# Chunked attention and a gated MLP in one kernel: all turned-block copies placed behind the sigmoid, and a new written order of the opening

## The chip, the cores and the metric

One NeuronCore of a Trainium2 chip. The metric is the device time of one launch in microseconds (us), as the median of several runs; the profile is of one more launch, which has its own time.

## The reference

Inputs are q, k, v of shape (8, 8, 576, 64) and three weights. Attention is within chunks of 64 tokens; its output, as 4608 tokens of 512 numbers, goes through a gated layer.

```python
scores = scale * np.matmul(q_c, k_c.transpose(0, 1, 2, 4, 3))      # chunks of 64 tokens
scores = scores - np.max(scores, axis=-1, keepdims=True)
attn = np.exp(scores)
attn = attn / (np.sum(attn, axis=-1, keepdims=True) + 1e-09)
x = np.matmul(attn, v_c)                                           # then (4608, 512)
gate = 1.0 / (1.0 + np.exp(-(x @ w_gate)))                         # (4608, 1536)
val = x @ w_val
return (gate * val @ w_out).astype(np.float32)
```

## The kernel before, in words

The 4608 tokens are 9 blocks of 512. Blocks 0 to 2 go through the gated layer tile by tile; blocks 3 to 8 go in three pairs with fewer products per pair (the functions from `product` to `outward`), and are not touched here. The hidden size 1536 is 12 tiles of 128. Each block has two attention pairs; a pair covers 256 tokens, with u in {0, 1} naming its two halves and i in {0, 1} the two heads side by side.

Numbers are kept in two parts, high and low (`hi`, `lo`, or `h` and `l`), each of TensorE's fast 32-bit type; a product is three passes. The weights arrive as 64-bit floats and are converted on the chip: ScalarE's `a` (two scalings, L145 and L146), VectorE's `t`, `b`, `d` (L148, L150, L153), ScalarE's `h` (L155), VectorE's `l` (L159), for gate (part 0), value (part 1), both at once (part u, "wide") or output weights (part 2) of tile f. A weight load is `w.f.part` (L118), 512 KB on SP's queue. Staging buffers are shared: a later load waits until the conversion of an earlier one has read its buffer.

**Opening.** Block 0 and the first two tiles of block 1 follow a written order, the string OPENING. Each token is one step, and every engine and SP's queue take their instructions in that order (`begin`). `q.p`, `v.p` load queries and keys (two DMAs) and values of pair p. `scores.p` are the products of pair p; `max`, `neg`, `sub` are VectorE's, and there are two ways to the exponential: `exp` is one ScalarE activation behind VectorE's `sub` and in front of VectorE's `sum`; `each` (L263) is eight activations with the maximum as bias and their sums read out, so that neither `sub` nor `sum` is needed. `inv` and `mul` scale. `turn.p.u` transposes on TensorE, `ca`, `ce` (ScalarE) or `cd` (VectorE) copy half of a turned block out (L287), `av.p` multiplies with the values (L211), `xh` (ScalarE) and `xl` (VectorE) split the result into x. `fill.n` are n products of no use, which keep TensorE busy (L101). `G.n.s` and `V.n.s` are gate and value products of tile n (n counts through the blocks, 12 per block) for tokens a (first half), b (second) or f (all), `g` is the sigmoid, `m` the gating product, `hh` and `hl` the two parts of the hidden tile, `D` its product with the output weights.

**Blocks 1 and 2.** `rest` calls `step` for each tile: `hidden` issues the gate products, the sigmoid (L372), the value products, VectorE's product `hf` (L375), ScalarE's cast `hx` (L378) and VectorE's remainder (L380). `finish` issues the output product of the tile before. Between them a planner, `tick` and `insert`, walks through the generator `flow`, which has the attention of later pairs: its items have a price, and move on as credit is given per tile. A pair's exponentials are one activation (L787), and its blocks are turned by VectorE (L814) in pieces that 16 copies of 32 x 256 (L825) put in place: 5 on POOL at once, and 11 for ScalarE into the list `held`. `release` issues what is held:

```python
    def release(most=16):
        for one in held[:most]:
            one()
        del held[:most]
```

It is called in `hidden` behind the sigmoid, with 5, and behind the cast `hx`, with all that are left; `insert` calls it too, ahead of `av` (`values2`, L211). VectorE also adds weights for the later pairs (L451, `keep_sums`), POOL works on (L460 to L465), SP stores. The finished block's output is copied by VectorE and ScalarE (L409, L407) and sent (L410).

Of the kernel before, what the change touches and what calls it, by code (L numbers as in the profile page):

```python
# [26 lines left out]


OPENING = """
w.1.1 w.0.0 q.0 w.0.1 q.1 w.1.0 a.1.1 v.0 a.0.0 t.1.1 b.1.1 t.0.0 d.1.1 b.0.0 h.1.1 fill.21 scores.0 d.0.0 l.1.1  # L30
h.0.0 max.0.0 a.0.1 neg.0.0 max.0.1 each.0.0 neg.0.1 l.0.0 t.0.1 fill.11 scores.1 b.0.1 each.0.1 inv.0.0 mul.0.0
max.1.0 max.1.1 a.1.0 d.0.1 neg.1.0 sub.1.1 w.2.1 each.1.0 w.0.2 inv.0.1 w.2.0 mul.0.1 w.1.2 t.1.0 fill.17 turn.0.1
q.2 b.1.0 turn.0.0 cd.0.1 ca.0.1 cd.0.0 ca.0.0 inv.1.0 exp.1.1 av.0 d.1.0 h.0.1 sum.1.1 h.1.0 v.1 l.0.1 xh.0.0.1
xh.0.1.0 w.3.0 xl.0.0.1 xh.0.1.1 xh.0.0.0 xl.0.1.1 a.0.2 xl.0.0.0 xl.0.1.0 inv.1.1 fill.9 G.0.a a.2.u mul.1.1 l.1.0
V.0.a mul.1.0 t.0.2 b.0.2 turn.1.0 d.0.2 turn.1.1 g.0.a ca.1.0 G.1.a m.0.a w.2.2 ce.1.0 t.2.u w.3.1 ca.1.1 ce.1.1
b.2.u hh.0.a av.1 h.0.2 a.1.2 l.0.2 V.1.a hl.0.a xh.1.0.1 t.1.2 xh.1.1.1 xl.1.0.1 g.1.a D.0.a xl.1.1.1 xh.1.0.0
xh.1.1.0 m.1.a xl.1.0.0 hh.1.a xl.1.1.0 a.3.u hl.1.a G.0.b d.2.u b.1.2 V.0.b g.0.b h.2.u d.1.2 t.3.u G.1.b w.3.2
h.1.2 w.4.1 m.0.b l.2.u hh.0.b w.4.0 a.2.2 V.1.b l.1.2 hl.0.b D.1.a b.3.u g.1.b a.3.2 m.1.b G.2.f d.3.u hh.1.b
hl.1.b w.5.0 h.3.u t.2.2 w.5.1 b.2.2 a.4.u D.0.b l.3.u d.2.2 scores.2 t.3.2 g.2.f t.4.u V.2.f h.2.2 b.4.u a.5.u
d.4.u G.3.f m.2.f w.6.0 max.2.0 w.6.1 h.4.u q.3 max.2.1 hh.2.f l.4.u V.3.f hl.2.f sub.2.1 g.3.f t.5.u b.3.2 G.4.f  # L40
m.3.f exp.2.1 b.5.u a.6.u sum.2.1 neg.2.0 D.1.b d.3.2 each.2.0 inv.2.1 w.5.2 mul.2.1 V.4.f d.5.u l.2.2 h.3.2 w.7.1
hh.3.f w.7.0 inv.2.0 mul.2.0 v.2 D.2.f h.5.u w.4.2 l.3.2 hl.3.f a.5.2 l.5.u turn.2.0 t.6.u D.3.f b.6.u g.4.f a.7.u
m.4.f t.5.2 b.5.2 G.5.f hh.4.f d.6.u a.4.2 hl.4.f h.6.u d.5.2 V.5.f t.4.2 w.7.2 h.5.2 l.6.u w.8.0 g.5.f ce.2.0 b.4.2
ca.2.0 l.5.2 G.6.f m.5.f d.4.2 hh.5.f t.7.u w.6.2 h.4.2 w.8.1 hl.5.f a.7.2 turn.2.1 l.4.2 D.5.f b.7.u ca.2.1 ce.2.1
g.6.f d.7.u a.6.2 av.2 t.7.2 b.7.2 h.7.u t.6.2 D.4.f b.6.2 a.8.u l.7.u d.6.2 V.6.f d.7.2 w.8.2 h.6.2 t.8.u w.9.2
h.7.2 l.6.2 xh.2.0.1 xh.2.1.1 b.8.u xh.2.1.0 xh.2.0.0 G.7.f m.6.f d.8.u hh.6.f a.8.2 hl.6.f w.10.1 V.7.f l.7.2 w.9.0
g.7.f w.10.0 xl.2.0.0 h.8.u w.9.1 xl.2.1.0 xl.2.1.1 w.11.1 l.8.u D.6.f m.7.f xl.2.0.1 hh.7.f t.8.2 hl.7.f a.9.0
b.8.2 D.7.f t.9.0 b.9.0 d.9.0 a.9.1 d.8.2 G.8.f h.9.0 w.10.2 t.9.1 h.8.2 v.3 l.9.0 b.9.1 a.9.2 d.9.1 V.8.f g.8.f
t.9.2 l.8.2 h.9.1 l.9.1 b.9.2 a.10.0 scores.3 d.9.2 m.8.f h.9.2 G.9.f t.10.0 hh.8.f b.10.0 d.10.0 l.9.2 h.10.0 V.9.f
hl.8.f a.10.1 l.10.0 max.3.1 a.10.2 t.10.1 b.10.1 D.8.f g.9.f t.10.2 b.10.2 d.10.2 d.10.1 w.11.0 h.10.2 G.10.f m.9.f  # L50
q.4 h.10.1 l.10.2 hh.9.f l.10.1 a.11.1 hl.9.f neg.3.1 V.10.f t.11.1 g.10.f b.11.1 a.11.0 d.11.1 t.11.0 w.11.2 h.11.1
b.11.0 D.9.f d.11.0 m.10.f each.3.1 l.11.1 max.3.0 V.11.f sub.3.0 h.11.0 inv.3.1 hh.10.f l.11.0 exp.3.0 hl.10.f
a.11.2 G.11.f sum.3.0 inv.3.0 t.11.2 mul.3.0 mul.3.1 D.10.f b.11.2 d.11.2 g.11.f h.11.2 m.11.f turn.3.0 l.11.2
hh.11.f G.12.a ca.3.0 hl.11.f cd.3.0 turn.3.1 g.12.a D.11.f ca.3.1 cd.3.1 av.3 v.4 ev.1 ev.2 ev.0 ev.3 V.12.a
xh.3.1.1 xh.3.0.1 xl.3.1.1 xh.3.1.0 xl.3.0.1 xh.3.0.0 G.13.a xl.3.0.0 m.12.a xl.3.1.0 hh.12.a hl.12.a V.13.a g.13.a
G.12.b m.13.a hh.13.a hl.13.a V.12.b g.12.b D.12.a m.12.b V.13.b hh.12.b hl.12.b D.12.b G.13.b D.13.a g.13.b m.13.b
hh.13.b hl.13.b
"""

# [933 lines left out]
```

## Time and profile before

| what | value |
|---|---|
| three runs | 901.86, 905.09, 906.74 us; median 905.09 |
| the profiled execution, its own time | 902.03 us |
| its span | 900.2 us |
[...]
| TensorE busy | 98% of the span |
| VectorE, ScalarE, POOL busy | 69%, 46%, 30% |

The span is from the first to the last recorded instruction. Engines are PE (TensorE), PEld (its weight loads), DVE (VectorE), ACT (ScalarE), POOL (GpSimd) and SP, whose queue issues the DMAs. In a row of a timeline, like instructions that follow each other are merged; the us are from the first start to the last end, and the bracket is the engine's idle time before the row with what ended it. "L825" is line 825 of the kernel.

### The profile page before, as it was taken

What the parts mean: (1) busy time and instruction counts of PE and PEld (TensorE: products, weight loads), DVE (VectorE), ACT (ScalarE), POOL (GpSimd) and SP (SyncE); (2) the same over time, 40 slices, a digit from 0 to 9 for tenths busy, and PEclk for the clock granted to TensorE, in tenths of its full rate; (3) what the DMA queues carried; (4) which work ended last, traced back from release to release, by engine and by line L of the source; (5) the groups of instructions that cost most, each with busy time, mean ns of one, the idle gap of its engine ahead of it and who ended that gap; (6) DMA issues with size and microseconds to landing.
All of it is one profiled execution on the core that took longest, in us unless ns stands there. A gap on an engine that the chain in (4) does not pass through costs nothing.

```text
span 900.2 us, 15612 instructions
## 1 busy us (share of the span) xinstructions
PE 882.1 (98%) x6054; PEld 720.3 (80%) x6054; DVE 618.8 (69%) x882; ACT 412.0 (46%) x738; POOL 272.4 (30%) x337
## 2 busy tenths in 40 slices
PE   7999999999999999999999999999999999999998
PEld 4887788887877878888888888887788888888886
DVE  6999882586665966666658976666679853435884
ACT  7887672355524463355544524455246221122341
POOL 0000000397846990267750001253500002432000
PEclk9999999999998999999999999999999999999999
DMA  8899962336354475588775567665446685564553
GB/s 312 305 338 297 353 195 71 131 129 190 131 166 148 142 221 177 171 278 284 257 277 187 210 231 283 234 234 190 163 160 224 211 283 197 183 204 150 187 210 117
DMA packets 84506, 189.77 MB, mean 211 GB/s; under 512 B 7248, under 2 KB 45648, under 8 KB 80592
## 3 DMA queue, kind: packets, MB, share of 16 engines
q1 hardware_dynamic: 84432, 188.77, 61.2%
q8 instruction: 48, 0.79, 0.4%
q14 instruction: 26, 0.21, 0.1%
HBM read 146.28 MB, written 42.47 MB: 210 GB/s over the span
## 4 chain that ended last, share of the span: by engine, by line
PE 81%; DVE 7%; ACT 4%; POOL 3%; issue 2%; DMA 2%; SPq 0%; POOLq 0%; DVEq 0%; ACTq 0%
PE d L699 19%; PE g L356 16%; PE cy L550 15%; PE cx L550 11%; PE cz L550 10%; PE acc L391 7%; PE av L211 2%; PE sc L196 2%; DMA w_raw<-w_in 2%; POOL pt L825 1%; ACT early L263 1%; ACT pt L825 1%; POOL a_val L465 1%; DVE xc L540 1%; DVE w_raw L153 1%
## 5 line engine op out<-in xcount | busy, mean ns | idle before, releaser
L356 PE MATMUL g<-xt,w 128*128 128x512 f32 (+1 forms) x960 | 208.1, 372 | 1.0 <-ACT hf L312 0.5
L356 PEld LDWEIGHTS g<-xt,w 128*128 128x128 f32 x960 | 168.5, 190 | 34.1 <-ACT hf L312 1.5
L699 PE MATMUL d<-hd,wd 128*128 128x512 f32 x756 | 172.5, 389 | 0.1
L699 PEld LDWEIGHTS d<-hd,wd 128*128 128x128 f32 x756 | 141.7, 188 | 30.3 <-DVE hd L679 0.9
L550 PE MATMUL cy<-xc,wr 128*128 128x512 f32 x648 | 159.4, 389 | 1.2 <-DVE s1u L568 1.2
L550 PEld LDWEIGHTS cy<-xc,wr 128*128 128x128 f32 x648 | 121.6, 188 | 26.8 <-DVE s1u L568 1.6
L550 PE MATMUL cx<-xc,wr 128*128 128x512 f32 x432 | 111.0, 392 | 0.6 <-issue 0.6
L550 PE MATMUL cz<-xc,wr 128*128 128x512 f32 x432 | 110.0, 390 | 0.2
L391 PE MATMUL acc<-w,hx 128*128 128x512 f32 x432 | 106.7, 394 | 0.1
L550 PEld LDWEIGHTS cz<-xc,wr 128*128 128x128 f32 x432 | 80.9, 188 | 17.8 <-issue 1.0
L550 PEld LDWEIGHTS cx<-xc,wr 128*128 128x128 f32 x432 | 80.5, 188 | 18.0 <-issue 1.0
L391 PEld LDWEIGHTS acc<-w,hx 128*128 128x128 f32 x432 | 79.7, 188 | 17.7 <-DVE hx L322 0.8
L825 POOL COPY pt<-pr 32x256 f32<-32x256 f32 x94 | 39.7, 423 | 163.9 <-DVE pr L814 154.8
L460 POOL TENSOR_TENSOR a_val<-a_val 128x128 f32<-128x128 f32 x36 | 19.0, 527 | 217.9 <-DVE a_val L451 167.5
L678 ACT CAST hd<-hid 128x1024 fp32r<-128x1024 f32 x48 | 49.9, 1052 | 49.2 <-PE d L699 33.2
L566 ACT COPY s1u<-cx 128x512 f32<-128x512 f32 x36 | 21.1, 587 | 106.3 <-PE cx L550 106.3
L679 DVE TENSOR_TENSOR hd<-hid,hd 128x1024 fp32r<-128x1024 f32 x48 | 58.3, 1221 | 12.4 <-ACT hd L678 12.2
L578 POOL TENSOR_TENSOR hid<-u,hid 128x512 f32<-128x512 f32 x15 | 19.3, 1285 | 142.4 <-DVE u L607 141.7
L825 ACT COPY pt<-pr 32x256 f32<-32x256 f32 x130 | 52.4, 403 | 10.5 <-DVE pr L814 8.6
L568 DVE TENSOR_TENSOR s1u<-cy,s1u 128x512 f32<-128x512 f32 x36 | 24.7, 685 | 39.9 <-PE cy L550 35.4
L628 ACT ACTIVATE hid<-hid 128x512 f32<-128x512 f32 x54 | 32.4, 628 | 35.3 <-DVE hid L622 29.3
L578 POOL TENSOR_TENSOR hid<-s1u,hid 128x512 f32<-128x512 f32 x30 | 41.1, 1379 | 20.8 <-DVE s1u L622 20.2
(118 smaller groups left out, 1118.4 us busy)
## 6 DMA issues: line engine op xcount, KB each, us to landing
wr<-sums SPq DMA_DIRECT2D x72, 512.0 KB, 4.8
wd<-stream SPq DMA_DIRECT2D x30, 1024.0 KB, 4.6
w_raw<-w_in SPq DMA_DIRECT2D x36, 512.0 KB, 5.2
wr<-given SPq DMA_DIRECT2D x36, 512.0 KB, 3.8
qt<-q_in SPq DMA_DIRECT2D x18, 512.0 KB, 4.8
kt<-k_in SPq DMA_DIRECT2D x18, 512.0 KB, 5.7
vt<-v_in SPq DMA_DIRECT2D x18, 512.0 KB, 4.7
given<-w SPq DMA_DIRECT2D x36, 256.0 KB, 5.6
```

The costliest lines, as they stand in the source:

```text
L356: nc.tensor.matmul(ps[:, tok], lhsT=wt[f, which][:, wpart, c:c + P], rhs=x[:, part, i, tok], start=n == 0, stop=n == 11)
L391: nc.tensor.matmul(acc[m, t], lhsT=hx[:, ts], rhs=wt[f, 2][:, wpart], start=f == 0 and i == 0, stop=f == NF - 1 and i == 2,)
L460: nc.gpsimd.tensor_tensor(out=val[:, 1], in0=val[:, 1], in1=val[:, 2], op=ALU.add)
L550: nc.tensor.matmul(bank, lhsT=lhs(wpart, c), rhs=x[:, part, c], start=start and k == 0, stop=stop and k == 5, skip_group_check=True)
L566: nc.scalar.copy(s1, x)
L568: nc.vector.tensor_tensor(out=u2, in0=y, in1=s1, op=ALU.add)
L578: eng.tensor_tensor(out=h, in0=value, in1=h, op=ALU.mult)
L628: nc.scalar.activation(h, h, AF.Sigmoid)
L678: nc.scalar.copy(t[:, 0], at)
L679: nc.vector.tensor_tensor(out=t[:, 1], in0=at, in1=t[:, 0].bitcast(F32), op=ALU.subtract)
L699: nc.tensor.matmul(bank, lhsT=w[:, o:o + P], rhs=x[:, part], start=p == 0 and opening and i == 0, stop=p == 5 and i == 2, skip_group_check ...
L825: copy = (lambda eng, dst=pb[dst, :, c, i, :], src=ps[src, h::2, k, :]: eng(dst, src))
```

## The change

Two edits. In `hidden`, the call behind the sigmoid releases all held copies instead of five. And OPENING is another order of nearly the same tokens. Removed: `cd.0.0`, `cd.0.1`, `cd.3.0`, `cd.3.1`, `neg.1.0`, `each.1.0`, `sub.1.1`, `exp.1.1`, `sum.1.1`, `sub.2.1`, `exp.2.1`, `sum.2.1`, `neg.3.1`, `each.3.1`, `fill.17`, `fill.9`. Added: `ce.0.0`, `ce.0.1`, `ce.3.0`, `ce.3.1`, `sub.1.0`, `exp.1.0`, `sum.1.0`, `neg.1.1`, `each.1.1`, `neg.2.1`, `each.2.1`, `sub.3.1`, `exp.3.1`, `sum.3.1`, `fill.13`, `fill.5`, `fill.15`. Tile 0 is loaded first, then tile 2, then tile 1; the loads of tile 4 stand ahead of those of value weights 3, those of 6 ahead of 5. The old order begins with value weights 1. Both turns of pair 1 come before G.0.a instead of behind V.0.a; pair 3's second turn comes behind D.11.f.

```diff
@@ OPENING @@
-w.1.1 w.0.0 q.0 w.0.1 q.1 w.1.0 a.1.1 v.0 a.0.0 t.1.1 b.1.1 t.0.0 d.1.1 b.0.0 h.1.1 fill.21 scores.0 d.0.0 l.1.1
-h.0.0 max.0.0 a.0.1 neg.0.0 max.0.1 each.0.0 neg.0.1 l.0.0 t.0.1 fill.11 scores.1 b.0.1 each.0.1 inv.0.0 mul.0.0
-max.1.0 max.1.1 a.1.0 d.0.1 neg.1.0 sub.1.1 w.2.1 each.1.0 w.0.2 inv.0.1 w.2.0 mul.0.1 w.1.2 t.1.0 fill.17 turn.0.1
-q.2 b.1.0 turn.0.0 cd.0.1 ca.0.1 cd.0.0 ca.0.0 inv.1.0 exp.1.1 av.0 d.1.0 h.0.1 sum.1.1 h.1.0 v.1 l.0.1 xh.0.0.1
-xh.0.1.0 w.3.0 xl.0.0.1 xh.0.1.1 xh.0.0.0 xl.0.1.1 a.0.2 xl.0.0.0 xl.0.1.0 inv.1.1 fill.9 G.0.a a.2.u mul.1.1 l.1.0
-V.0.a mul.1.0 t.0.2 b.0.2 turn.1.0 d.0.2 turn.1.1 g.0.a ca.1.0 G.1.a m.0.a w.2.2 ce.1.0 t.2.u w.3.1 ca.1.1 ce.1.1
-b.2.u hh.0.a av.1 h.0.2 a.1.2 l.0.2 V.1.a hl.0.a xh.1.0.1 t.1.2 xh.1.1.1 xl.1.0.1 g.1.a D.0.a xl.1.1.1 xh.1.0.0
-xh.1.1.0 m.1.a xl.1.0.0 hh.1.a xl.1.1.0 a.3.u hl.1.a G.0.b d.2.u b.1.2 V.0.b g.0.b h.2.u d.1.2 t.3.u G.1.b w.3.2
-h.1.2 w.4.1 m.0.b l.2.u hh.0.b w.4.0 a.2.2 V.1.b l.1.2 hl.0.b D.1.a b.3.u g.1.b a.3.2 m.1.b G.2.f d.3.u hh.1.b
-hl.1.b w.5.0 h.3.u t.2.2 w.5.1 b.2.2 a.4.u D.0.b l.3.u d.2.2 scores.2 t.3.2 g.2.f t.4.u V.2.f h.2.2 b.4.u a.5.u
...
-a.11.2 G.11.f sum.3.0 inv.3.0 t.11.2 mul.3.0 mul.3.1 D.10.f b.11.2 d.11.2 g.11.f h.11.2 m.11.f turn.3.0 l.11.2
-hh.11.f G.12.a ca.3.0 hl.11.f cd.3.0 turn.3.1 g.12.a D.11.f ca.3.1 cd.3.1 av.3 v.4 ev.1 ev.2 ev.0 ev.3 V.12.a
-xh.3.1.1 xh.3.0.1 xl.3.1.1 xh.3.1.0 xl.3.0.1 xh.3.0.0 G.13.a xl.3.0.0 m.12.a xl.3.1.0 hh.12.a hl.12.a V.13.a g.13.a
-G.12.b m.13.a hh.13.a hl.13.a V.12.b g.12.b D.12.a m.12.b V.13.b hh.12.b hl.12.b D.12.b G.13.b D.13.a g.13.b m.13.b
-        release(5)
+w.0.0 w.0.1 q.0 w.0.2 q.1 a.0.0 a.0.1 t.0.0 b.0.0 t.0.1 d.0.0 b.0.1 h.0.0 fill.21 scores.0 d.0.1 l.0.0 w.2.0 h.0.1
+w.2.1 max.0.0 a.0.2 w.1.0 neg.0.0 max.0.1 v.0 each.0.0 w.1.1 neg.0.1 t.0.2 l.0.1 b.0.2 fill.11 scores.1 d.0.2
+each.0.1 inv.0.0 w.2.2 mul.0.0 max.1.0 max.1.1 a.2.u inv.0.1 mul.0.1 sub.1.0 fill.13 turn.0.1 neg.1.1 turn.0.0
+exp.1.0 t.2.u ca.0.0 sum.1.0 ce.0.0 ca.0.1 b.2.u ce.0.1 each.1.1 fill.5 av.0 inv.1.0 mul.1.0 v.1 d.2.u q.2 xh.0.0.1
+xh.0.0.0 inv.1.1 w.1.2 xh.0.1.0 xl.0.0.0 xh.0.1.1 mul.1.1 a.1.0 xl.0.1.1 xl.0.0.1 a.1.1 xl.0.1.0 t.1.0 fill.15
+turn.1.0 b.1.0 turn.1.1 ce.1.0 ca.1.0 G.0.a d.1.0 ce.1.1 t.1.1 h.1.0 b.1.1 ca.1.1 V.0.a d.1.1 l.1.0 w.3.0 av.1 g.0.a
+w.4.0 h.1.1 m.0.a w.4.1 h.0.2 l.1.1 G.1.a xh.1.1.1 l.0.2 xh.1.0.0 hh.0.a xh.1.0.1 hl.0.a xh.1.1.0 V.1.a xl.1.0.1
+g.1.a xl.1.1.0 a.1.2 xl.1.1.1 xl.1.0.0 D.0.a m.1.a h.2.u t.1.2 b.1.2 G.0.b hh.1.a a.2.2 hl.1.a l.2.u V.0.b g.0.b
+d.1.2 a.4.u t.2.2 w.3.2 G.1.b m.0.b w.3.1 b.2.2 d.2.2 V.1.b hh.0.b h.1.2 hl.0.b t.4.u g.1.b h.2.2 G.2.f l.1.2 m.1.b
+a.3.2 b.4.u a.3.u d.4.u D.1.a t.3.2 w.6.1 b.3.2 D.0.b w.6.0 h.4.u t.3.u b.3.u hh.1.b V.2.f d.3.u hl.1.b w.5.1 h.3.u
+l.4.u scores.2 w.5.0 g.2.f l.3.u D.1.b a.6.u m.2.f G.3.f l.2.2 d.3.2 hh.2.f hl.2.f w.5.2 h.3.2 a.5.u l.3.2 V.3.f
+max.2.0 max.2.1 neg.2.0 neg.2.1 g.3.f t.5.u D.2.f b.5.u each.2.1 m.3.f d.5.u G.4.f t.6.u w.7.1 hh.3.f w.4.2 inv.2.1
+each.2.0 hl.3.f b.6.u V.4.f d.6.u h.5.u inv.2.0 w.8.1 mul.2.0 q.3 D.3.f l.5.u g.4.f w.8.0 a.4.2 w.7.0 mul.2.1 v.2
+m.4.f w.11.1 h.6.u t.4.2 G.5.f b.4.2 hh.4.f d.4.2 a.5.2 hl.4.f w.6.2 l.6.u h.4.2 turn.2.1 g.5.f V.5.f t.5.2 ce.2.1
...
+d.11.0 D.9.f m.10.f h.11.0 v.3 l.11.1 hh.10.f l.11.0 sub.3.1 V.11.f hl.10.f a.11.2 sub.3.0 t.11.2 b.11.2 G.11.f
+exp.3.0 d.11.2 exp.3.1 sum.3.0 h.11.2 inv.3.0 sum.3.1 l.11.2 D.10.f mul.3.0 inv.3.1 mul.3.1 g.11.f m.11.f G.12.a
+hh.11.f hl.11.f turn.3.1 g.12.a D.11.f ce.3.1 ca.3.1 turn.3.0 ev.0 ev.1 V.12.a ce.3.0 ev.2 ca.3.0 ev.3 av.3 v.4
+m.12.a hh.12.a hl.12.a G.13.a xh.3.0.1 xh.3.1.0 xl.3.0.1 xh.3.1.1 xl.3.1.0 xh.3.0.0 xl.3.1.1 V.13.a g.13.a xl.3.0.0
...
@@ hidden @@
@@ -370,7 +370,7 @@
         pg = up(m, f, 0, tok)
         hf = mp.tile([P, TB], F32, name="hf", bufs=1)[:, tok]
         nc.scalar.activation(hf, pg, AF.Sigmoid)
-        release(5)
+        release()
         pv = up(m, f, 1, tok)
         nc.vector.tensor_tensor(out=hf, in0=pv, in1=hf, op=ALU.mult)
         both = mp.tile([P, 2, TB], F32R, name="hx")
```

## Rows read from the trace of the kernel before

**Rows 1.** The page, part 1: busy us (share of the span) and instructions of each engine.

```profile
PE 882.1 (98%) x6054; PEld 720.3 (80%) x6054; DVE 618.8 (69%) x882; ACT 412.0 (46%) x738; POOL 272.4 (30%) x337
```

**Rows 2.** Waits of PE, 200 to 350 us: total us, times, longest.

```profile
PE av L211 <- ACT pt L825: 5.6, 6, 3.8
```

**Rows 3.** Timeline of PE, block 2: start, us, engine, line, op, [idle before <- releaser].

```profile
267.66 0.34 PE L211 MATMUL av<-pt,vt 64*64 64x64 f32 x8
271.85 0.44 PE L211 MATMUL av<-pt,vt 64*64 64x64 f32 x2 [3.84 <-ACT pt L825]
272.59 1.76 PE L211 MATMUL av<-pt,vt 64*64 64x64 f32 x54 [0.30 <-ACT pt L825]
274.29 7.59 PE L356 MATMUL g<-xt,w 128*128 128x512 f32 x24
...
299.44 1.16 PE L211 MATMUL av<-pt,vt 64*64 64x64 f32 x64
300.54 3.02 PE L391 MATMUL acc<-w,hx 128*128 128x512 f32 x12
```

**Rows 4.** Timeline of ACT (ScalarE), two pairs of blocks 1 and 2.

```profile
206.99 2.07 ACT L825 COPY pt<-pr 32x256 f32<-32x256 f32 x5
210.01 0.62 ACT L378 CAST hx<-hf 128x512 fp32r<-128x512 f32 x1 [0.95 <-DVE hf L375]
...
263.90 2.07 ACT L825 COPY pt<-pr 32x256 f32<-32x256 f32 x5
269.42 0.62 ACT L378 CAST hx<-hf 128x512 fp32r<-128x512 f32 x1 [3.44 <-DVE hf L375]
270.06 2.48 ACT L825 COPY pt<-pr 32x256 f32<-32x256 f32 x6
```

**Rows 5.** Timeline of DVE (VectorE), around the wait in block 2.

```profile
256.43 0.69 DVE L409 COPY ob<-acc 128x512 f32<-128x512 f32 x1 [7.39 <-PE sc L196]
...
268.70 0.68 DVE L375 TENSOR_TENSOR hf<-g,hf 128x512 f32<-128x512 f32 x1
```

**Rows 6.** Windows: us, busy of PE, PEld, DVE, ACT, POOL, granted clock, DMA share, GB/s.

```profile
25.00:60.00 35.00, 34.40 (x316) 30.07 (x316) 33.42 (x57) 29.48 (x52) 0.00 (x0) 1.00 0.93 312
...
272.00:278.00 6.00, 5.70 (x65) 4.62 (x65) 2.28 (x3) 5.23 (x9) 5.48 (x9) 0.50 0.34 114
```

**Rows 7.** Timeline of PE, the last pair of block 1.

```profile
211.82 0.34 PE L211 MATMUL av<-pt,vt 64*64 64x64 f32 x8
...
214.16 5.74 PE L356 MATMUL g<-xt,w 128*128 128x512 f32 x24
```

**Rows 8.** Timeline of SP (DMA issues), before the wait in block 2.

```profile
251.57 6.59 SPq L410 DMA_DIRECT2D out<-ob  x4
```

**Rows 9.** Timeline of DVE, lead-in.

```profile
15.85 0.69 DVE L252 TENSOR_REDUCE mx<-sc 128x8 f32<-128x512 f32 x1 [0.64 <-ACT early L263]
...
17.73 0.16 DVE L269 TENSOR_SCALAR sums<-sums 128x8 f32<-128x8 f32 x1
```

**Rows 10.** Timeline of ACT, copies of pair 1's turned blocks.

```profile
29.05 1.20 ACT L287 COPY pt<-tp 128x256 f32<-128x256 f32 x4
```

**Rows 11.** Timeline of PE, lead-in and first products.

```profile
21.31 1.16 PE L211 MATMUL av<-pt,vt 64*64 64x64 f32 x64 [1.25 <-ACT pt L287]
...
24.28 3.54 PE L356 MATMUL g<-xt,w 128*128 128x256 f32 x24
27.65 1.04 PE L280 MATMUL tp<-ident,early 128*128 128x128 f32 x8
29.20 1.69 PE L356 MATMUL g<-xt,w 128*128 128x256 f32 x12 [0.52 <-ACT hf L312]
```

**Rows 12.** The chain of waits, in order of time, first 40 us.

```profile
0.74 4.01 DMA w_raw<-w_in
...
18.25 2.48 ACT early L263 x16
```

**Rows 13.** Timeline of SP, lead-in.

```profile
17.21 1.77 SPq L118 DMA_DIRECT2D w_raw<-w_in  x4
```

More of the change, by code (lines that the diff above doesn't have):

```diff
@@ L40 @@
[L40 to L49, printed above, removed]
@@ L50 @@
-hl.8.f a.10.1 l.10.0 max.3.1 a.10.2 t.10.1 b.10.1 D.8.f g.9.f t.10.2 b.10.2 d.10.2 d.10.1 w.11.0 h.10.2 G.10.f m.9.f
-q.4 h.10.1 l.10.2 hh.9.f l.10.1 a.11.1 hl.9.f neg.3.1 V.10.f t.11.1 g.10.f b.11.1 a.11.0 d.11.1 t.11.0 w.11.2 h.11.1
-b.11.0 D.9.f d.11.0 m.10.f each.3.1 l.11.1 max.3.0 V.11.f sub.3.0 h.11.0 inv.3.1 hh.10.f l.11.0 exp.3.0 hl.10.f
-a.11.2 G.11.f sum.3.0 inv.3.0 t.11.2 mul.3.0 mul.3.1 D.10.f b.11.2 d.11.2 g.11.f h.11.2 m.11.f turn.3.0 l.11.2
-hh.11.f G.12.a ca.3.0 hl.11.f cd.3.0 turn.3.1 g.12.a D.11.f ca.3.1 cd.3.1 av.3 v.4 ev.1 ev.2 ev.0 ev.3 V.12.a
@@ new lines @@
+m.4.f w.11.1 h.6.u t.4.2 G.5.f b.4.2 hh.4.f d.4.2 a.5.2 hl.4.f w.6.2 l.6.u h.4.2 turn.2.1 g.5.f V.5.f t.5.2 ce.2.1
+l.4.2 ca.2.1 b.5.2 a.8.u d.5.2 w.7.2 G.6.f m.5.f a.7.u t.8.u b.8.u D.4.f hh.5.f t.7.u h.5.2 hl.5.f a.6.2 l.5.2 b.7.u
+g.6.f D.5.f a.7.2 d.7.u d.8.u h.7.u turn.2.0 V.6.f w.10.0 l.7.u ce.2.0 w.9.0 ca.2.0 t.6.2 h.8.u b.6.2 d.6.2 G.7.f
+m.6.f w.8.2 h.6.2 l.8.u w.9.1 hh.6.f l.6.2 a.9.0 av.2 hl.6.f t.7.2 g.7.f t.9.0 V.7.f b.7.2 a.8.2 d.7.2 b.9.0 a.9.1
+d.9.0 G.8.f h.7.2 m.7.f xh.2.0.1 t.9.1 hh.7.f l.7.2 xh.2.1.0 hl.7.f h.9.0 xh.2.0.0 t.8.2 V.8.f g.8.f b.8.2 xh.2.1.1
@@ new lines @@
+d.8.2 xl.2.1.0 w.10.2 h.8.2 b.9.1 w.9.2 w.10.1 D.6.f d.9.1 l.8.2 h.9.1 m.8.f l.9.1 xl.2.1.1 a.10.0 V.9.f xl.2.0.1
+xl.2.0.0 l.9.0 hh.8.f t.10.0 a.9.2 hl.8.f b.10.0 D.8.f t.9.2 d.10.0 b.9.2 h.10.0 d.9.2 scores.3 l.10.0 h.9.2 a.10.2
+l.9.2 G.9.f max.3.0 a.10.1 t.10.2 b.10.2 d.10.2 D.7.f t.10.1 w.11.0 g.9.f b.10.1 h.10.2 d.10.1 m.9.f h.10.1 l.10.2
+G.10.f hh.9.f l.10.1 a.11.1 hl.9.f max.3.1 a.11.0 t.11.1 V.10.f b.11.1 g.10.f t.11.0 d.11.1 b.11.0 w.11.2 h.11.1 q.4
+d.11.0 D.9.f m.10.f h.11.0 v.3 l.11.1 hh.10.f l.11.0 sub.3.1 V.11.f hl.10.f a.11.2 sub.3.0 t.11.2 b.11.2 G.11.f
@@ L57 @@
+exp.3.0 d.11.2 exp.3.1 sum.3.0 h.11.2 inv.3.0 sum.3.1 l.11.2 D.10.f mul.3.0 inv.3.1 mul.3.1 g.11.f m.11.f G.12.a
+hh.11.f hl.11.f turn.3.1 g.12.a D.11.f ce.3.1 ca.3.1 turn.3.0 ev.0 ev.1 V.12.a ce.3.0 ev.2 ca.3.0 ev.3 av.3 v.4
+m.12.a hh.12.a hl.12.a G.13.a xh.3.0.1 xh.3.1.0 xl.3.0.1 xh.3.1.1 xl.3.1.0 xh.3.0.0 xl.3.1.1 V.13.a g.13.a xl.3.0.0
+G.12.b m.13.a hh.13.a hl.13.a V.12.b g.12.b D.12.a m.12.b V.13.b hh.12.b hl.12.b D.12.b D.13.a G.13.b g.13.b m.13.b
 hh.13.b hl.13.b
```

## Prediction

> **What bounds the kernel now.** I read the page's busy times first. TensorE is busy for 882.1 us of 900.2 [rows 1], so the time moves only with what TensorE does not need: idle time, a lower clock, and the lead-in before its first useful product. The waits of TensorE between 200 and 350 us come next [rows 2]: the whole list there is one line, `av` (attention times values) waiting for ScalarE's turned copies `pt`, 5.6 us in six waits, the longest 3.8. The copies belong to blocks 1 and 2, where each of six pairs sends 11 copies to ScalarE.
>
> The worst wait is in TensorE's order of time [rows 3]. `av` starts at 267.66, runs 8 products, stands 3.84 us, runs 2 more, and does the other 54 from 272.59. ScalarE's order shows why [rows 4]: 5 copies run behind the sigmoid from 263.90, ending at 265.97; then ScalarE holds nothing but the cast `hx`, which waits 3.44 us for VectorE's product `hf` at 268.70 [rows 5]; the last 6 copies stand behind it and run from 270.06 to 272.54. Their data were there when the first five ran. [...]
>
> **The price of that stall.** With nothing late, `av` takes 1.10 us to the next product (299.44 to 300.54 [rows 3]). Here it takes 274.29 - 267.66 = 6.63, so 5.53 are lost. The 24 gate and value products behind it last 7.59 us, against 5.74 in the same place of an undisturbed clock [rows 3, 7]: 1.85 more. Together 7.38 us. The same pattern, much milder, stands at 211.82 (next product 214.16, that is 2.34 instead of 1.10, 1.24 lost [rows 7]) and once more at the last pair of block 2, equal in size. The other three pairs lose nothing. In all 9.86 us.
>
> **Part one, all copies behind the sigmoid.** No instruction is added; six copies of each pair move ahead of `hx` on ScalarE. A copy comes every 0.41 us (five in 2.07, six in 2.48 [rows 4]), so 11 need 4.57. At the stall they end at 263.90 + 4.57 = 268.47. Unstalled, `av` would be done at 268.76; with its last 54 products after 268.47, at the pace in which the undisturbed 64 take 1.10 us, it is done at about 269.46. That leaves 0.70, and saves 6.68. At 206.99 + 4.57 = 211.56 the copies are all done before `av` at 211.82: the 1.24 go wholly, twice. **Sum -9.16 us.**
>
> What it delays: `hx` and, through it, VectorE's `hx` remainder (L380) and the weight sums (L451) queued behind that. In the usual pair, as at 206.99, `hx` starts when the 11 copies end, 211.56, instead of 210.01 [rows 4]: 1.6 us later. Its reader, the down product of that step, comes after the next step's 24 products (5.74 us), so this costs nothing while that cover stands; without it, 1.6 us each, six times. At 267 nothing is delayed at all, since the copies fit into the 3.44 us for which ScalarE stood. POOL's five copies of a pair, SP's queue and the exponential behind the copies keep their places. What is late next at 267 is still VectorE: it stood 7.39 us before the copy of block 1's output at 256.43 [rows 5], because the buffer of the copy before it was still being sent (issued at 251.57 [rows 8]).
>
> **Part two, the opening.** First, what it is not: `each` (ScalarE's eight exponentials with sums) stands five times in the old order (0.0, 0.1, 1.0, 2.0, 3.1) and five times in the new (0.0, 0.1, 1.1, 2.0, 2.1). Only four VectorE copies `cd` become ScalarE's `ce`. Real TensorE work, 12 hidden tiles and their products, is the same; the 58 fills become 65, all ahead of the first product and in its waiting time.
>
> Step by step to the first product. The inverse of pair 0 came at 17.73, after the maximum at 15.85 (which waited for `each.0.1`) and three steps of other work [rows 9]; in the new order it follows the maximum directly, about 16.46: 1.27 earlier, and so the turns, 17.7. Against this ScalarE now does one whole exponential (behind `sub.1.0`, to about 18.95) and four copies (1.20 for four [rows 10]): about 20.2 for `av.0`, against 21.31 [rows 11]. Then `each.1.1`, 2.48 [rows 12], stands ahead of the casts `xh`, and ends near 22.7; the turns of pair 1 stand ahead of G.0.a and need its inverse and scaling, which VectorE has behind a wide conversion step: about 24.6. With turns of 1.04, G.0.a starts at about 25.7 instead of 24.28, 1.4 later. But the 1.04 of turns that came at 27.65 are then done, and the wait of 0.52 at 29.20 [rows 11] should go: 1.4 - 1.04 - 0.52 = -0.2. I take **-0.2 us**.
>
> The same edits once more, in pairs 2 and 3: pair 2 now has both its exponentials as `each` (2.48 instead of one activation, on a ScalarE that is busy 29.48 of 35 us [rows 6]), pair 3 both as `exp`; each pair's second turn comes later, pair 3's with V.12.a between it and `av.3`, so that its two copies (0.6 [rows 10]) may look out by that much. All of it lies beside 12 tiles' products: 0, or +0.6.
>
> On the price of `each.1.1` the row shows 16 instructions in 2.48 us [rows 12]. [...]
>
> The queues. SP: w.2.0 and w.2.1 go out once `d.0.1` is done, which now comes ahead of the first maximum (an estimate: near 9), where in the old order SP sat until 17.21 with four weight loads [rows 13]; v.0 becomes the eleventh load instead of the ninth. The first landed at 4.75 [rows 12]; at the 312 GB/s of 25 to 60 us [rows 6] a load of 512 KB takes 1.7 us and the eleventh lands near 21.6, 1.4 after it is wanted; at a better rate it is hidden. I take 0 and keep +1.4. v.1 now goes out ahead of q.2, w.1.2 and w.3.0 and, waiting for `av.0`, holds them; these are wanted many us later. POOL's queue gets nothing. From 25 us on VectorE is busy for 33.42 of 35 us [rows 6], so it is the second bound; by a count of its steps along both written orders, the new one has more of them ahead of tiles 1 to 3 (pair 1's scaling, the wide conversion of tile 4) and fewer from tile 5 on. Bounds of the opening: -1.5 (the lead of 1.1 at `av.0` kept, and half a wait) to +6.5 (rival 1).
>
> **Sum.** The profiled execution took 902.03 us, 3.06 under the median of 905.09. 902.03 - 9.16 - 0.2 = 892.7. Whether the other runs' 3 us come from deeper forms of these stalls, which go, or from elsewhere, no row tells; I add half: **894 us**.
>
> **Rivals.**
> 1. *The opening gives part back.* Tile 3's weights are now loaded and converted behind tile 4's (w.4.0, w.4.1 ahead of w.3.1). With VectorE at 33.42 of 35 [rows 6] little slack is left at G.3.f. One wait like the worst seen, 3.84 with the clock's 1.85 and 0.77 on the 54 products behind it (1.70 from 272.59 to 274.29, for 54/64 of 1.10 [rows 3]), costs 6.5: 900.5. For it: the order; against it: the loads of tile 2 start some 8 us sooner [rows 13]. Chance 0.17, about 0.10 of it under 900.6.
> 2. *The stall shrinks, but stays.* VectorE's 7.39 us before 256.43 ends with an output transfer, not with TensorE [rows 5, 8]. If that keeps its time while TensorE comes 1.24 + 0.2 earlier, `av` waits 0.7 + 1.4 = 2.1; should the clock fall as well (1.85 + 0.77), 4.0 of the gain are gone: 898. Against: the stores ahead of that transfer are paced by TensorE's own steps. Chance 0.12.
> 3. *Slower.* The same order as in rival 1 decides at tiles 3, 5 and 7, whose loads stand behind those of 4, 6 and (half) 8: VectorE late by one wide conversion at each gives three waits. At 6.5 each, 19 us: 913. It decides from about 4.6 us per wait (three of them eat the 9.4 gained and the 4.5 that count). Against: the old order ran the same work with TensorE busy 34.40 of 35 us [rows 6]. Chance 0.06.
> 4. *The change does not do what it says.* If `av` waits for POOL's copies and not ScalarE's, moving these changes nothing: 905. Against: TensorE restarts at 271.85 and 272.59, the second 0.05 us after the last ScalarE copy's end [rows 3, 4]. Chance 0.05.
>
> **The numbers.** The forecast has 0.60. About 0.5%, 4.5 us, is what a measurement of this kernel can tell from no change, so faster means under 900.6. Faster: 0.60 + 0.10 + 0.12 = 0.82. The same: 0.07 + 0.05 = 0.12. Slower: 0.06. The range runs from 889 (opening at -1.5, no offset, no rest at 267, and 1.5 for runs) to 901 (rivals 1 and 2, offset kept), and leaves out the rest of 1, and 3 and 4.
>
> **What would show it.** Right: 11 ScalarE copies in one run behind each sigmoid of blocks 1 and 2, `hx` behind them; no `av` wait on `pt` over 1 us between 200 and 350; clock 1.00 there; G.0.a near 25.7 and no TensorE wait over 1 us up to tile 12. Wrong: a wait of TensorE for weights or VectorE before tiles 3 to 7; the 3.84 us reappearing elsewhere in blocks 1 and 2; a clock of 0.50 anywhere before 350 us.

## The result and the profile after

The changed kernel takes 895.6 us, the median of five runs (892.79 to 897.8), against 905.09 before: ratio 0.990, interval 0.9865 to 0.9936. Forecast were 894.0 us, in 889 to 901, and faster by over 0.5%. The profiled execution took 892.79 us, with a span of 891.0 (before: 902.03 and 900.2); the sum of the forecast for it was 892.7. TensorE's busy time, from the page of the changed kernel, fell by 3.1 us against [rows 1], although seven more fills are in it:

```profile
PE 879.0 (99%) x6061; PEld 719.0 (81%) x6061; DVE 619.6 (70%) x878; ACT 413.3 (46%) x742; POOL 275.0 (31%) x337
```

The waits of TensorE between 200 and 350 us, the view of [rows 2]: 5.6 us in six waits of `av` became one of 0.5, and a wait for the sigmoid is new.

```profile
PE g L356 <- ACT hf L372: 1.1, 1, 1.1
PE av L211 <- ACT pt L825: 0.5, 1, 0.5
```

TensorE's timeline there (start, duration, line, tile, count, idle time before and its releaser):

```profile
210.83 1.16 PE L211 MATMUL av<-pt,vt 64*64 64x64 f32 x64
211.92 5.74 PE L356 MATMUL g<-xt,w 128*128 128x512 f32 x24
...
265.40 0.45 PE L211 MATMUL av<-pt,vt 64*64 64x64 f32 x10
266.30 1.04 PE L211 MATMUL av<-pt,vt 64*64 64x64 f32 x54 [0.45 <-ACT pt L825]
267.27 5.74 PE L356 MATMUL g<-xt,w 128*128 128x512 f32 x24
...
312.34 1.59 PE L211 MATMUL av<-pt,vt 64*64 64x64 f32 x64
...
339.69 5.53 PE L356 MATMUL g<-xt,w 128*128 128x512 f32 x23 [1.06 <-ACT hf L372]
```

At the long stall `av` now takes 267.27 - 265.40 = 1.87 us to the next product instead of 6.63, and the 24 products behind it 5.74 instead of 7.59 [rows 3]: 4.76 + 1.85 = 6.61. The windows give TensorE's granted clock, as a share of full speed: 1.00, where it was 0.50 [rows 6].

```profile
264.00:270.00 6.00, 5.55 (x83) 4.38 (x82) 5.28 (x8) 4.96 (x9) 5.19 (x8) 1.00 0.27 90
```

ScalarE's timeline shows the eleven copies in one run behind each sigmoid, `hx` behind them, and the last cast ahead of the new wait:

```profile
205.99 4.58 ACT L825 COPY pt<-pr 32x256 f32<-32x256 f32 x11
...
261.67 4.58 ACT L825 COPY pt<-pr 32x256 f32<-32x256 f32 x11
267.18 0.62 ACT L378 CAST hx<-hf 128x512 fp32r<-128x512 f32 x1 [0.93 <-DVE hf L375]
...
308.26 4.57 ACT L825 COPY pt<-pr 32x256 f32<-32x256 f32 x11
...
338.09 1.05 ACT L532 CAST xc<-raw 128x1024 fp32r<-128x1024 f32 x1 [4.30 <-DVE raw L528]
```

VectorE's timeline shows that its own wait stayed, 7.96 us for 7.39 [rows 5], and that the copy behind it and the product `hf` both come 2.23 us earlier than before (256.43 and 268.70), as TensorE does by 2.26 (265.40 for 267.66). At 336.85 it is late with block 3's `raw`, for which ScalarE's cast above waits.

```profile
254.20 0.69 DVE L409 COPY ob<-acc 128x512 f32<-128x512 f32 x1 [7.96 <-PE sc L196]
...
266.47 0.68 DVE L375 TENSOR_TENSOR hf<-g,hf 128x512 f32<-128x512 f32 x1
...
336.85 2.35 DVE L528 TENSOR_TENSOR raw<-raw 128x1024 f32<-128x1024 f32 x2
```

In the opening, TensorE's timeline comes close to the steps of the forecast: `av.0` at 19.40 (forecast 20.2), pair 1's turns at 24.68 (24.6), G.0.a at 25.50 (25.7); the wait of 0.52 [rows 11] is gone.

```profile
19.40 1.44 PE L211 MATMUL av<-pt,vt 64*64 64x64 f32 x64
...
24.68 1.06 PE L280 MATMUL tp<-ident,early 128*128 128x128 f32 x8 [0.50 <-DVE xt L300]
25.50 3.11 PE L356 MATMUL g<-xt,w 128*128 128x256 f32 x24
```

ScalarE's timeline has `each.1.1`, eight exponentials with eight accumulator reads, up to the next work (first and last rows):

```profile
19.49 0.35 ACT L263 ACTIVATE early<-sc,mx 128x64 f32<-128x64 f32 x1
...
21.73 0.28 ACT L263 ACTIVATION_READ_ACCUMULATOR early<-sc,mx 128x1 f32 x1
21.82 1.27 ACT L298 CAST xt<-av 128x256 fp32r<-128x256 f32 x4
```

Matched by event, the changed kernel leads by 0.99 us at block 1's first scores (155.23 against 156.22), 8.71 at the first scores of the stage behind block 2 (375.51 against 384.22), and 9.2 at the end.

### The profile page after: what moved, and what is told of

It reads as the page before. It is cut to its first block, busy times and chain, and to the rows that moved or that the text cites. A ratio compares the mean times of both kernels' runs of the same rounds, so it can differ in the third digit from the quotient of the medians.

```text
span 891.0 us, 15627 instructions
## 1 busy us (share of the span) xinstructions
PE 879.0 (99%) x6061; PEld 719.0 (81%) x6061; DVE 619.6 (70%) x878; ACT 413.3 (46%) x742; POOL 275.0 (31%) x337
## 4 chain that ended last, share of the span: by engine, by line
PE 72%; DVE 10%; ACT 7%; DMA 5%; issue 3%; POOL 2%; SPq 0%; POOLq 0%; ACTq 0%; DVEq 0%
PE d L699 19%; PE cy L550 15%; PE cx L550 10%; PE cz L550 10%; PE g L356 10%; PE acc L391 5%; DMA w_raw<-w_in 3%; PE av L211 2%; ACT pt L825 1%; PE sc L196 1%; DVE w_raw L153 1%; ACT early L263 1%; DVE hx L380 1%; POOL pt L825 1%; DVE xc L540 1%
## 5 line engine op out<-in xcount | busy, mean ns | idle before, releaser
L356 PEld LDWEIGHTS g<-xt,w 128*128 128x128 f32 x960 | 166.7, 188 | 33.7 <-ACT hf L372 1.5
L568 DVE TENSOR_TENSOR s1u<-cy,s1u 128x512 f32<-128x512 f32 x36 | 24.6, 684 | 40.1 <-PE cy L550 35.6
L578 POOL TENSOR_TENSOR hid<-s1u,hid 128x512 f32<-128x512 f32 x30 | 41.0, 1377 | 20.8 <-DVE s1u L622 20.2
```

What stands on the lines that cost most here:

```text
L356: nc.tensor.matmul(ps[:, tok], lhsT=wt[f, which][:, wpart, c:c + P], rhs=x[:, part, i, tok], start=n == 0, stop=n == 11)
L568: nc.vector.tensor_tensor(out=u2, in0=y, in1=s1, op=ALU.add)
L578: eng.tensor_tensor(out=h, in0=value, in1=h, op=ALU.mult)
```

## The experiments

The theory is that of the forecast: the release behind the sigmoid gives nearly all, through the long stall. The rivals are that the opening gives it, or that VectorE's late output sets the stall and not the order of the copies. Twelve experiments follow, two of them repeats, in three groups; each group shares its runs of the kernel before (medians 903.43, 903.64 and 903.37 us).

**One part at a time.** The release alone is the kernel before with

```
-        release(5)
+        release()
```

> The old opening, with all 11 copies behind the sigmoid. Theory (the copies' place is nearly the whole gain): the waits of av on pt between 200 and 350 us fall from 5.6 us to about 1, the granted clock stays 1.00 there, and the time falls by 9.2 us less what is given back later (0.9 in the changed kernel): 902.0 - 8.3 = about 894 in the profiled run, ratio to before 0.99. Rival (the new opening shifts the phases of VectorE and POOL, and with them the stall goes; the copies' place matters little): about 900 to 902, with the long wait of av still near 268 us.

Measured 896.78 us, ratio 0.9921 (0.9903 to 0.9938). TensorE's waits from 200 to 350 us are those of the changed kernel:

```profile
PE g L356 <- ACT hf L372: 1.0, 1, 1.0
PE av L211 <- ACT pt L825: 0.4, 1, 0.4
```

The opening alone is the changed kernel with `release(5)` put back.

> The new opening, with 5 copies behind the sigmoid and 6 behind the cast as before. Theory: the opening is ahead by 1.0 us at the end of tile 0's first output product and still at the last pair of block 1, and no more; the 3.8 us wait of av near 267 us and the clock of 0.50 behind it stand: 901 in the profiled run, ratio 0.998 to 0.999. Rival (phases shift): 893, ratio 0.99, and no wait over 1 us near 267.

Measured 904.07 us, ratio 1.0001 (0.998 to 1.0021), with the waits of before:

```profile
PE av L211 <- ACT pt L825: 5.5, 5, 3.8
```

So the release is worth the whole change, and the opening nothing that this measurement shows.

**The dose.** The kernel before with no copy behind the sigmoid, so that all eleven follow `hx`:

```
-        release(5)
+        pass
```

> The kernel before with no copy behind the sigmoid: all 11 behind the cast, the suspected cost doubled. Theory: at each of the three pairs that stall the last copy ends five copies later, 2.1 us each, 6.2 in all: 908; at the two mild pairs the wait grows from 0.7 to nearly 3 us, and if the clock falls there too, another 2.6 each: up to 913. The three pairs without a stall have 5 to 9 us to spare and stay without. Rival (what av waits for is not these copies): 902, waits as before.

Measured 912.56 us, ratio 1.0103 (1.0073 to 1.0132). TensorE's timeline shows `av` broken at the long stall, and again at both pairs that lost 1.24 us before (213.92 and 328.27):

```profile
276.28 0.90 PE L211 MATMUL av<-pt,vt 64*64 64x64 f32 x8 [2.87 <-POOL a_high L464]
278.42 0.44 PE L211 MATMUL av<-pt,vt 64*64 64x64 f32 x2 [1.24 <-ACT pt L825]
279.16 1.77 PE L211 MATMUL av<-pt,vt 64*64 64x64 f32 x54 [0.30 <-ACT pt L825]
```

The view names POOL for the first of these waits, but POOL's five copies of the pair had ended at 268.69. By its own timeline ScalarE makes its eleven from 274.54 to 279.11; TensorE's first two restarts fall within that time, and the last comes 0.05 us behind it:

```profile
274.54 4.57 ACT L825 COPY pt<-pr 32x256 f32<-32x256 f32 x11
```

The clock fell at both mild pairs too (24 products took 7.43 and 6.70 us, for 5.74), so the time lies at the upper end of what was expected. None, five and eleven copies ahead of `hx` give 912.6, 903.4 and 896.8 us: the order of the copies decides. The other three pairs stay free even with none.

**What makes VectorE late.** The kernel before with block 1's four output transfers issued from ScalarE's queue, so that they no longer stand on SP behind the stores of the weight sums (L468):

```
-        nc.sync.dma_start(rows, ob)
+        (nc.scalar if m == 1 else nc.sync).dma_start(rows, ob)
```

> The kernel before with the four output transfers of block 1 issued from ScalarE's queue and not from SP's, nothing else. Theory of the root (VectorE is late at 268 because its copy of block 1's output waits for a buffer that SP, held by the stores of POOL's sums, sends late): VectorE's 7.4 us before the copy near 256 shrink to about 3, hf comes at 265.5 and not 268.7, the cast and six copies end about 3 us earlier, av's wait falls from 3.84 to about 1 with the clock at 1.00: about 896. Rival (VectorE is late of its own load, scores and weight sums): hf still 3 to 4 us behind TensorE, the wait stays, 901 to 903.

Measured 898.54 us, ratio 0.995 (0.9934 to 0.9965). VectorE's 7.39 us [rows 5] are 2.23:

```profile
253.47 0.69 DVE L409 COPY ob<-acc 128x512 f32<-128x512 f32 x1 [2.23 <-DMA out<-ob]
```

and `av` stands twice 0.45 instead of 3.84, the clock at 1.00 from 270 to 280 us (windows; the rows are TensorE's timeline):

```profile
270.88 0.30 PE L211 MATMUL av<-pt,vt 64*64 64x64 f32 x2 [0.45 <-ACT pt L825]
271.62 1.04 PE L211 MATMUL av<-pt,vt 64*64 64x64 f32 x54 [0.45 <-ACT pt L825]
...
320.62 7.32 PE L356 MATMUL g<-xt,w 128*128 128x512 f32 x24
```

The time stayed 2.5 us above the 896 expected: the two mild pairs still wait, and behind the last one the clock fell (24 products in 7.32 us, for 5.74). So the long stall has two keys, either of which opens it: VectorE late because a buffer was still being sent, and six copies that stood behind its product for no need. The change turns the second.

**Where does the opening's lead go?** To settle this the changed kernel and the release alone ran side by side.

> The changed kernel once more, beside the next run, which has the release alone. If the new opening keeps its lead of 1.0 to 2 us (scores of block 1 at 155.2 in the changed kernel's profile, at 156.2 to 157.5 with the old opening), this run is 1 to 2 us under the release alone, about 895.2 against 896.8. If the lead is given back later, as the run of the opening alone suggests by its time of 904.1 against 903.4, the two agree within 0.7 us.

> The release alone once more (before with release() in place of release(5)). About 896.8 by both theories, and 0.992 of the kernel before; the profile of its opening tells whether TensorE's clock falls to 0.50 between 20 and 26 us (first gate product near 25.6, scores of block 1 near 157.5) or not (24.3 and 156.2).

Measured 897.21 (0.9918, 0.9899 to 0.9937) and 895.86 us (0.9914, 0.9896 to 0.9932): the changed kernel is 1.35 above, which neither case expected. With the first runs, the median of eleven runs of the changed kernel is 896.99, that of twelve of the release alone 896.33. So the opening is worth nothing that these times show, yet it leads. A table of all profiles, cut at two events that each has, shows why (us; the first scores of block 1, the first scores behind block 2, the end of the span; "wait" is the one for nothing that the profile shows, near 605 us):

| kernel | opening, fills | to scores 1 | from there to scores 2 | to the end | wait, and where |
|---|---|---|---|---|---|
| before | old, 58 | 156.22 | 228.00 | 516.0 | 0.56, behind 5 cx |
| none behind the sigmoid | old, 58 | 157.13 | 236.81 | 517.5 | 1.10, behind 5 cx |
| outputs on ScalarE's queue | old, 58 | 158.98 | 223.50 | 517.5 | 1.64, behind 5 cx |
| release alone | old, 58 | 157.53 | 220.24 | 517.9 | 1.37, behind 5 cx |
| release alone, again | old, 58 | 157.02 | 220.41 | 517.1 | 1.61, behind 5 cx |
| release, values later | old, 58 | 159.16 | 220.28 | 517.8 | 0.72, behind 5 cx |
| release, 5 fills ahead of av.0 | old, 63 | 157.51 | 220.10 | 519.9 | 3.00, behind 0 cx |
| changed | new, 65 | 155.23 | 220.28 | 515.5 | none |
| changed, again | new, 65 | 156.66 | 219.30 | 520.0 | 2.73, 3 scores left |
| opening alone | new, 65 | 155.34 | 228.32 | 522.1 | 2.99, 3 scores left |
| changed, outputs on ScalarE | new, 65 | 160.79 | 217.87 | 521.5 | 3.02, 3 scores left |
| changed, values later | new, 65 | 155.06 | 220.11 | 519.1 | 3.00, 3 scores left |
| changed, both | new, 65 | 155.58 | 217.94 | 518.3 | 2.74, 3 scores left |
| changed, 7 fewer fills | new, 58 | 156.10 | 220.24 | 517.3 | 1.60, behind 4 cx |

In the kernels that leave the outputs on SP, the middle column goes by the order of the copies alone: 236.8 us with none behind the sigmoid, 228.0 and 228.3 with five, 219.3 to 220.4 with all. The release is worth 7.8 us (228.0 - 220.2). The first column is the opening: the median of seven is 157.5 with the old one and 155.6 with the new, 1.9 us of lead. The third gives it back: 517.5, the median of the seven kernels with 58 fills, against 519.6, that of the six with 65. What differs is above all the wait in the last column. It stands at a place in TensorE's instructions, not at a piece of work: each fill more moves it up by one product, from behind five `cx` (58 fills) to behind none (63). With 65 it falls among the short scores. Counted among the recorded products, it stands behind 4753 of them in every profile with the old opening, with 58 fills or 63, and behind 4752 in every one with the new, with 58 or 65. Behind it the clock fell in some of the profiles. TensorE's timelines of before, of the changed kernel run again, and of the kernel with 63 fills:

```profile
610.18 1.43 PE L550 MATMUL cx<-xc,wr 128*128 128x512 f32 x5
612.17 0.50 PE L550 MATMUL cx<-xc,wr 128*128 128x512 f32 x1 [0.56 <-issue]
```

```profile
600.87 1.10 PE L196 MATMUL sc<-kt,qt 64*64 64x64 f32 x61
604.70 0.33 PE L196 MATMUL sc<-kt,qt 64*64 64x64 f32 x3 [2.73 <-issue]
...
606.64 2.76 PE L550 MATMUL cz<-xc,wr 128*128 128x512 f32 x6
```

```profile
606.60 2.07 PE L550 MATMUL cx<-xc,wr 128*128 128x512 f32 x6 [3.00 <-issue]
608.47 2.74 PE L550 MATMUL cz<-xc,wr 128*128 128x512 f32 x6
```

The reader should see the six `cz` at 2.76 and 2.74 us, where an undisturbed row has 1.52: a lower clock. The windows around these rows grant 0.57 as a mean from 606 to 610 us in the one, and 0.62 from 608 to 612 in the other.

The mean clock granted to each run is on record as well. Of the eleven runs of the changed kernel, the five at 0.999 or more took 892.8 to 895.6 us, and the six below that 897.0 to 897.8. Of the twelve of the release alone, seven at 0.999 or more took 892.9 to 896.8, the five others 895.2 to 898.4. Where the clock holds, the changed kernel is thus 2.6 us ahead by medians (893.3 against 895.9), and where it falls it is not (897.7 against 897.5). These are few runs, and for those without a profile it is not known where the clock fell.

**The fill ahead of av.0** belongs to another question, whether the clock decides the old opening. It fell to 0.50 in the release alone (windows, 22 to 24 us); `av.0` took 1.99 us for 1.16, and G.0.a started at 25.63 instead of 24.28 [rows 11] (TensorE's timeline):

```profile
21.25 1.99 PE L211 MATMUL av<-pt,vt 64*64 64x64 f32 x64 [1.24 <-ACT pt L287]
...
25.63 3.22 PE L356 MATMUL g<-xt,w 128*128 128x256 f32 x24
```

The edit, on the release alone:

```
-... exp.1.1 av.0 d.1.0 ...
+... exp.1.1 fill.5 av.0 d.1.0 ...
```

> The release alone, and in the old opening five more fills in TensorE's order ahead of av.0, in a wait of 1.24 us. If the old opening is slow because that wait makes the clock fall (av.0 1.99 us instead of 1.16, nine fills up to 4.0 instead of 2.1), the clock stays at 1.00 from 20 to 28 us, the first gate product starts at 24.3 to 24.5 instead of 25.6, and the time is 1.0 to 1.3 us under the release alone: 895.6. If the clock falls for the wait ahead of the turns already (1.5 us before 18.95), or the clock is not what delays it, the first gate product stays at 25.6 or later and the time at 896.8.

Measured 896.02 us (0.9922, 0.9905 to 0.9939), the same as the release alone. The clock stayed up (`av.0` in 1.16 us again, the nine fills behind it in 2.12 for 2.81) and G.0.a started in time:

```profile
21.40 1.16 PE L211 MATMUL av<-pt,vt 64*64 64x64 f32 x64 [0.17 <-ACT pt L287]
...
24.37 3.53 PE L356 MATMUL g<-xt,w 128*128 128x256 f32 x24
```

Still block 1's scores came at 157.51, as in the run with the late G.0.a (157.53). So the fallen clock of the lead-in is not what costs the old opening its 1.9 us; the expectation failed there. What the profiles with the old opening share, all but that of before, is a wait of tile products for ScalarE's `hf` (L312) near 75 us, 0.55 to 1.83; with the new opening none stands at that place. Whether this wait makes up the 1.9 us is not shown.

**Moving the wait.** The changed kernel with 58 fills:

```
-fill.21 ... fill.11 ... fill.13 ... fill.15
+fill.19 ... fill.9 ... fill.12 ... fill.13
```

> The changed kernel with seven of its 65 fills left out (fill.21, 11, 13 and 15 made 19, 9, 12 and 13), so that it has the old opening's 58. In the profiles so far TensorE's wait for nothing that is shown, near 605 us, stands behind the fifth cx product in every run with 58 fills (0.56 to 1.64 us), ahead of the first with 63 (3.00) and three scores earlier with 65 (2.7 to 3.0, or none), and in the last two the clock falls behind it. If the place in TensorE's instruction stream decides, it stands about five cx products in again, lasts 0.6 to 1.6 us, the clock stays at 1.00 there, and the median comes from 897.2 to about 895. If the work at that place decides, it stays in the scores at 2.7 to 3.0 us, and the time at 897. If the missing fills let the clock fall in the lead-in, the first gate product is late by 1 to 2 us and the time as much longer.

Measured 895.81 us (0.9919, 0.9901 to 0.9936). The wait moved by seven products, from three scores before the end to behind four `cx`, where five were expected, and shrank to 1.60:

```profile
602.32 1.19 PE L550 MATMUL cx<-xc,wr 128*128 128x512 f32 x4
605.12 0.61 PE L550 MATMUL cx<-xc,wr 128*128 128x512 f32 x2 [1.60 <-issue]
605.57 1.52 PE L550 MATMUL cz<-xc,wr 128*128 128x512 f32 x6
```

The clock held (six `cz` in 1.52, granted 1.00 from 602 to 612 us). The place is shown; the gain in time, 1.2 us under the pooled median of the changed kernel, is not more than the runs vary. Nor did the five fills added to the release alone show in the time (896.02 against 895.86).

**What it waits for.** The queues' view has an instruction transfer there. In the changed kernel's first profile, which had no wait, it is seen from 598 to 599 us, ahead of `av`; in the one with 2.73 us of wait from 602 to 603, within it (columns: queue, kind, packets, MB, share). First the one, then the other:

```profile
q8 instruction: 1, 0.02, 5.8%
```

```profile
q8 instruction: 1, 0.02, 5.8%
```

A load of 512 KB of values is issued just then, behind the `av` that reads the buffer (in the second of these profiles between 601 and 602 us, with `av` over at 601.05). To take it out of the way, the seven such loads of the later blocks were issued from ScalarE, behind the exponential (`load_values` takes the queue as an argument):

```
-                    load_values(j)
...
+                if joined:
+                    load_values(j, nc.scalar)
```

> The changed kernel, with the seven loads of values of the later blocks issued from ScalarE's queue behind the exponential, some 8 us after av, and no longer while TensorE works through 128 short products. If the wait near 605 us is for an instruction transfer that stands behind the 512 KB of values, it is gone or under 0.6 us, the clock stays at 1.00 from 600 to 620 us, and the runs lie near the fast ones of the changed kernel: 893.0 to 893.5. If the transfer of values has nothing to do with it, the wait of 2.7 to 3.0 us stays in most runs and the median at 895.6 to 897.2; if ScalarE's issues or the later values cost something, a wait of av or of ScalarE shows it, 1 to 3 us.

> The release alone, with the old opening, and the values loaded later in the same way. With the wait near 605 us gone in both, this run beside the one before it gives the opening's own worth: if the new opening leads by 1 to 2 us to the end (scores of block 1 at 155.2 to 156.7 against 156.2 to 157.5), this one takes 894.3 to 895.0 and the other 893.0 to 893.5. If the opening is worth nothing, the two agree within 0.7 us.

Measured 897.89 (0.9933, 0.9912 to 0.9955) and 897.12 us (0.9932, 0.9916 to 0.9947). The wait stayed:

```profile
604.81 0.33 PE L196 MATMUL sc<-kt,qt 64*64 64x64 f32 x3 [3.00 <-issue]
```

So the values are not its cause, and this theory fell; here the clock did not fall behind it (the next six `cz` took 1.54, granted 1.00 from 602 to 612 us). With the old opening the wait is 0.72, within the 0.56 to 1.64 of the other profiles with 58 fills.

That TensorE waits for its instructions fits the place that moves with each fill, and the transfers' times in the traces fit as well. In four profiles with the wait (before; changed, again; changed, values later; changed, 7 fewer fills), a 16 KB instruction transfer on q8 ends 1.3 to 1.6 us before TensorE goes on (at 603.13, with TensorE at 604.70, in the second view above). In the one without, it had ended at 598.99, 2.3 us before the product of the same number started. This is an argument from times: no run changed the transfer itself, and what makes it start late stays open.

**A version that goes on from the changed kernel** takes block 1's outputs off SP as well, first alone, then with the values later:

> The changed kernel, with block 1's four output transfers issued from ScalarE's queue. VectorE's wait before the copy near 254 falls from some 7 us to 2, so its product of the next step is in time and the 0.45 us of av near 266 go. If that wait is all that the late output still costs, 0.5 us under the changed kernel: 895.1. If the late output also causes later waits (1.06 us at 339.69), 1.5 under it: 894.1. If ScalarE's issues hold up its copies, up to 1 us above it: 896.6.

> All together: the changed kernel, values later, and block 1's four outputs issued from ScalarE's queue. The wait of av near 266 us (0.45) goes with the output, the wait near 605 us with the values. If both hold, 891.5 to 892.2, the range of the three fastest runs of the changed kernel with the output alone, in nearly all runs; if the two queues' issues on ScalarE hold up its copies, 893 to 895.

Measured 893.69 (0.9904, 0.9872 to 0.9935) and 894.53 us (0.9906, 0.9885 to 0.9927). In the second TensorE's timeline has `av` whole at the place of the long stall:

```profile
265.42 1.16 PE L211 MATMUL av<-pt,vt 64*64 64x64 f32 x64
```

and the wait of 1.06 at 339.69 is 0.3 in both. The middle column says 217.9 for both, 2.3 less than with the release alone. The medians lie 3.5 and 3.4 under those of the same kernels without it, in the same groups; the intervals overlap, so the gain is shown for the stage and only likely for the whole.

## Why the prediction was right, and where it was not

- **The long stall.** Forecast 6.68, measured 6.61. The copies end at 266.25, forecast as 4.57 us behind the sigmoid and measured at 4.58; the rest of 0.70 is 0.77 (1.87 - 1.10). The clock's 1.85 came back whole. This step carried the result.
- **The mild pairs.** The first gave 1.25, 1.24 in the forecast (211.92 - 210.83 = 1.09, and 2.34 before). The last pair of block 2 lost as much before, but gave back only 0.83: "the 1.24 go wholly, twice" failed there. The copies end at 312.83 and `av` starts at 312.34, so that it still takes 1.51 us, without a wait that the profile lists. The sigmoid ahead of the copies had waited 0.97 us for VectorE's remainder (L380), so they start 4.08 us ahead of `av`; before, it was 4.83 (316.29 and 321.12).
- **What is late next.** The text named VectorE at 267, and 0.45 us were left there. It did not price the next place: at 339.69 the gate products wait 1.06 us for ScalarE, and ScalarE for VectorE's `raw`; TensorE, 9 us earlier, catches VectorE's work on block 3, and 0.94 of the lead is gone (9.61 at 313.85, against 323.46 before; 8.67 at 339.69, against 348.36). So the release is worth 6.61 + 1.25 + 0.83 - 0.94 = 7.75, and not 9.16; the middle column says 7.7 for this pair of profiles (228.00 - 220.28).
- **Costs held to be nothing.** `hx` 1.6 us later in the usual pair cost nothing, as forecast: no wait stands behind it up to 339 us.
- **The opening.** G.0.a came within 0.2 of its forecast, and the load of v.0 held nothing. The turns ahead of G.0.a met their time by another step than the one priced. Pair 1's scaling (L273) was done at 23.87, and the turns began at 24.68 behind VectorE's `xl` (L300), which empties the buffers of `av.0` that the kernel uses again for the turns. `each.1.1` held ScalarE from 19.49 to the next work at 21.82, 2.33 us, and 2.52 to the end of its last read, which is how the row's 2.48 [rows 12] is measured. One exponential with its read follows another there every 0.29 us. But the sum of -0.2 was the wrong size for what follows: 1.9 us of lead by medians, 0.99 in the pair of profiles shown. In that pair 0.84 stands at the first output product (32.62 for 33.46): 0.33 from the steps priced (1.22 later, 1.55 of turns and wait gone), and the rest from the first tiles' products, which the forecast held equal (the first 24 took 3.11 us for 3.54). That the total was near -0.2 all the same is chance. The step that failed is "the 58 fills become 65, all ahead of the first product and in its waiting time": they cost no time there, but they move a wait 580 us later into a worse place, for 2.1 us by the medians of the table's last stage.
- **The sum and the offset.** 892.7 against 892.79 for the profiled execution is the sum of errors that cancel: 1.4 too much for the release (9.16 against 7.7), 0.8 too little for the opening, and 0.5 more at the end (515.5 against 516.0) in an execution that had no wait at 605 us. "I add half" of the 3.06 us failed: the runs differ in the first and the last column (155.1 to 160.8, 515.5 to 522.1), which the release doesn't touch, while the middle one repeats within 1.1. The whole offset should have been kept, 895.8, and 895.6 was measured. That agreement is in part luck too: the repeat gave 897.21 against 903.64, 6.4 us less and not 9.5. And the upper end of the range does not follow from its terms: rival 1 with the offset kept is 895.8 + 6.5 = 902.3, not 901.
- **The rivals.** The first, that the opening gives part back at tile 3, did not come: no wait over 0.5 us stands between the first gate product and tile 12 in the changed kernel's profile, and of the six others with this opening one has such waits (0.63 at 68.9, 1.82 at 103.6). It gives its lead back, but at 605 us. The second did not come either: the transfers were issued 2.01 us earlier (249.56 for 251.57) and VectorE's copy came 2.23 earlier, with TensorE's own steps, which was the argument against it. The third and fourth did not come.
